# The products x = kv q as six matmuls in natural layout, q split behind one float32 turn through DRAM, h in two banks

## Chip, cores, metric

One core of one Trainium2 chip runs the whole program. The metric is the device time in microseconds (us) of one execution; lower is better. Times below are of the kernel before the change.

## What is computed

The reference is an attention with its softmaxes taken apart, followed by an expert layer (8 batches, 8 heads, 576 positions, 64 columns a head; all float32):

```
q_s = softmax(q, axis=-1);  k_s = softmax(k, axis=2)      # k over the positions
kv  = einsum('bhsd,bhse->bhde', k_s, v)
x   = einsum('bhsd,bhde->bhse', q_s, kv)                  # -> 4608 tokens x 512
h   = x @ w_in                                            # 512 x 2048
g   = s * relu(h)**2 + b
out = g @ w_out                                           # 2048 x 512
```

## The kernel before

**Precision.** A float32 product is made of three products of rounded halves: a value is split into high (rounded to the matmul's type fp32r) and low (the rest), and high·high + high·low + low·high are added in a bank of PSUM.

**Tokens in blocks.** Each batch has 512 main tokens and 64 left ones; the left ones of the eight batches make a ninth block. Batch b's x is block b. The layer runs in steps t = 16·block + f: step t makes h (12 matmuls of 512 columns), TensorE's next 12 matmuls add the step before to the output ("o", written `acc`). Between h and o of a step stand, in this order, ACT's relu into `r`, DVE's square, ACT's `gh` and DVE's `gl`. `r` has one buffer and h one bank. Blocks 0 to 4 run so, in steps 0 to 79. Blocks 5 to 8 run as two pairs, with seven products of half size instead of eight (`bankU`, `bankV`); their x is staged first and cast into the weights' old places (`w<-stage`, b_cast).

**Attention under the layer.** Batches 0 and 1 are done at the start in another way. For batches 2 to 7 (units u = 8 to 31, two heads each; pr = u // 2) every unit's x is made between the layer's steps: `k_late`, `q_late`, `kv_late`, `x_late`. A unit's q passes through ACT's exp (tile `qe`, two buffers), DVE, GpSimd and a 32x32 transpose, then is split in two halves, both are written to DRAM (`turned`) and read back in another order into `spare` (`part()`, one buffer for all units), which TensorE reads. The two halves stand there side by side on 64 + 64 partitions, and one matmul over 128 partitions with 128 weight columns makes two partial sums of a head on the two halves of the output partitions; `evict` copies one half on ACT and adds the other on DVE. A unit takes four such matmuls (2 heads x 2 ranges of 320 and 256 columns).

**Where x goes.** For batches under AHEAD = 3, x is split straight into the layer's tile (`x_tile`). That of later ones goes to DRAM (`xs`); for batches 3 and 4, `x_back` reads it back in two pieces of 512 KB each, and ACT and DVE split it. The layer's tiles have two buffers, so block b's tile is free after h of step 16·(b-1) - 1.

**Order.** All engines execute in a fixed order, written by a planner (`Order`): each work item is an Op with an engine, a planned cost, a due time in steps, names it needs and gives, and buffers it takes and frees; `late=` adds an allowance in us to what it needs. An engine that reaches an instruction whose inputs aren't there waits, and so does all that stands behind it. `a_sums` (GpSimd sums of weights for the pairs) are due from DUE_S on, PACE_S steps apart.

Of the kernel before, what the change touches and what calls it, by code (L numbers as in the profile page):

```python
# [25 lines left out]
def attention_moe(ctx: ExitStack, tc: tile.TileContext, q, k, v, w_in, w_out, s, b, out):  # L26
    nc = tc.nc
# [16 lines left out]
    AHEAD = min(3, FIRST)  # L44
# [546 lines left out]
    def q_late(u):  # L591
# [64 lines left out]
    def kv_late(pr):  # L656
        us = (2 * pr, 2 * pr + 1)
        due = begin(pr)
        tag = "big" if paired(pr // 2) else "sm"
        yield Op("PE", 1.52, due - 200, needs=[f"k{u}" for u in us] + [f"v{pr} there"], take=[tag], gives=[f"kv{pr}"], late=WAIT)  # L660

        kt, _, vt = tiles[pr]
        kv = ps.tile([P, 2, 512], F32, name=f"kv_{pr}", tag="big")[:, 0] if tag == "big" else ps.tile([P, 512], F32, name=f"kv_{pr}", tag="sm", bufs=1)
        kv = kv[:, 0:2 * (D + 1)].rearrange("p (u e) -> p u e", u=2)
        heads(kv, by_head(kt).rearrange("p (u h) n d -> p u h n d", u=2), v_at(vt))
        yield Op("DVE", 0.5, due)
        z = small.tile([P, 2], F32, name=f"z_{pr}", tag="z")
        nc.vector.tensor_scalar(z, kv[:, :, D], 1e-9, None, op0=ALU.add)
        nc.vector.reciprocal(z, z)

        kvf = kvfs[pr % 2]
        for h in range(2):
            yield Op("DVE", 0.5, due, needs=[f"x{u - 4}" for u in us] if pr < NP + 2 else [f"kvhl{pr - 2}"], free=[tag] if h else ())
            for g in range(2):
                nc.vector.tensor_tensor(
                    out=kvf[half[g], :, h], in0=kv[half[h], :, 0:D], in1=z[half[h]].unsqueeze(2).to_broadcast([D, 2, D]),
                    op=ALU.mult
                )
        yield Op("ACT", 0.4, due, needs=["mid"] if pr == NP else [f"xp{2 * pr - 1}"])

        t = kv_part().rearrange("p u (a d) -> p u a d", d=D)
        nc.scalar.copy(t[:, :, 0:4:3], kvf)
        yield Op("POOL", 0.76, due, gives=[f"kvhl{pr}"])
        nc.gpsimd.tensor_tensor(out=t[:, :, 1:3], in0=kvf, in1=t[:, :, 0:4:3].bitcast(F32), op=ALU.subtract)

    def x_late(u):

        pr, i = divmod(u, 2)
        bb, hp = divmod(u, NP)
        due = begin(pr)  # L690
        narrow = paired(bb)
        L, M = NT * D, NQ * D
        width = (NT, NQ)
        qs = lambda: part().rearrange("p h (s a n c) -> p h s n a c", s=2, a=2, c=SQ)
        kvhl = lambda: kv_part()[:, i].rearrange("p (h e) -> p h e", h=2)

        def products(a, outs):
            for h in range(2):
                nc.tensor.matmul(outs[h], kvhl()[:, h], qs()[:, h, a, 0:width[a]], start=True, stop=True)

        def wide_bank(a):
            t = ps.tile([P, 2, 512], F32, name=f"xp_{u}_{a}", tag="big")
            return [t[:, h, 0:L] for h in range(2)] if a == 0 else [t[:, 0, h * M:(h + 1) * M] for h in range(2)]

        needs = [f"q{u}", f"kvhl{pr}"] + [f"y{u - 1}"] * i + ([f"h{NFC * (bb - 1) - 1}"] if bb < AHEAD else [])
        y = None

        def y_at(h, a):
            return y.rearrange("p (n s c) -> p s n c", s=2, c=D)[half[h], a, 0:width[a]]

        def spread_out(outs, h, a):
            return outs[h].rearrange("p (n c) -> p n c", c=D)

        def evict(a, outs, free):
            nonlocal y
            yield Op("ACT", (0.84, 0.74)[a], due, take=() if a else ["tmp", "soft"])
            y = y if y is not None else work.tile([P, 2 * L], F32, name=f"y_{u}", tag="tmp", bufs=NTMP)
            for h in range(2):
                nc.scalar.copy(y_at(h, a), spread_out(outs, h, a)[half[1 - h]])
            if not narrow and a == 0:  # L720
                return
            for a_ in ((0, 1) if not narrow else (a,)):
                yield Op("DVE", (0.98, 0.84)[a_], due, free=free if a_ == a else (), gives=[f"y{u}"] if a_ else ())
                for h in range(2):
                    nc.vector.tensor_tensor(
                        out=y_at(h, a_), in0=spread_out(parts[a_], h, a_)[half[h]], in1=y_at(h, a_), op=ALU.add
                    )

        parts = [None, None]
        if narrow:  # L730
            for a in range(2):
                yield Op("PE", 0.3, due - 200, needs=needs if a == 0 else (), take=["big"], gives=[f"xp{u}"] if a else (), late=WAIT if a == 0 else 0.0)
                parts[a] = wide_bank(a)
                products(a, parts[a])
                yield from evict(a, parts[a], ["big"])
        else:
            yield Op("PE", 0.57, due - 200, needs=needs, take=["big", "sm"], gives=[f"xp{u}"], late=WAIT)
            xq = ps.tile([P, 512], F32, name=f"xq_{u}", tag="sm", bufs=1)
            parts = [wide_bank(0), [xq[:, h * M:(h + 1) * M] for h in range(2)]]
            for h in range(2):  # L740
                for a in range(2):
                    nc.tensor.matmul(parts[a][h], kvhl()[:, h], qs()[:, h, a, 0:width[a]], start=True, stop=True)
            for a in range(2):
                yield from evict(a, parts[a], ["big", "sm"])
        if bb < AHEAD:
            xh, xl = [t[:, hp] for t in x_tile(bb)]
            yield Op("ACT", 0.58, due)
            nc.scalar.copy(xh, y[:, 0:TB])
            yield Op("DVE", 0.69, due, gives=[f"x{u}"])
            nc.vector.tensor_tensor(out=xl, in0=y[:, 0:TB], in1=xh.bitcast(F32), op=ALU.subtract)  # L750
            yield Op("SP", 0.4, due, kb=32, free=["tmp", "soft"], gives=[f"left{u}"])
            nc.sync.dma_start(xleft[:, hp, bb * LEFT:(bb + 1) * LEFT], y[:, TB:S])
        else:
            yield Op("SP", 0.4, due, kb=288, free=["tmp", "soft"], gives=[f"xs{u}", f"left{u}"] + [f"x{u}"] * (bb >= FIRST))
            nc.sync.dma_start(xs[bb][:, hp], y[:, 0:S])

    def x_back(bb, k):
# [7 lines left out]
        yield Op("ACT", 1.04, due, late=SLACK)  # L765
# [68 lines left out]
    def ring_loads():  # L834

        for i in range(len(PAIRS)):
            for p in range(HP):
                for m, k in enumerate(TURN):
# [3 lines left out]
                    needs += [f"kv{2 * FIRST + 1}" if ahead else f"h{FIRST * NFC - 1}"] * (i == 0)  # L842
# [568 lines left out]
```

## Time and profile before

| | us |
|---|---|
| three runs: median (lowest to highest) | 871.23 (868.63 to 871.85) |
| the profiled execution's own time | 870.1 |
| its span, first to last instruction | 868.2 |
| TensorE (PE) busy | 842.8 (97%) |
| VectorE (DVE) busy | 593.9 (68%) |
| ScalarE (ACT) busy | 439.7 (51%) |
| GpSimd (POOL) busy | 197.9 (23%) |

The span is 1.9 us shorter than the execution's own time; sums below are made on the span. TensorE works through a fixed list nearly without a break, so the time is its list's length plus its waits: a change shows where it lengthens the list and where it takes or adds a wait.

### The profile page before, as it was taken

The page shows a single profiled execution, that of the slowest core. Times are in us where ns is not written, and L with a number is a line of the kernel's source. Part 1 is how long each engine was busy: PE and PEld are TensorE (multiplying, and loading weights), DVE is VectorE, ACT ScalarE, POOL GpSimd, SP SyncE. Part 2 cuts the span into 40 slices and gives each one's busy share as a digit, 9 for nine tenths or more (in the row PEclk, how much of TensorE's full clock was granted, in tenths as well). Part 3 has the DMA queues.
Part 4 walks back from the last instruction along what each step waited for, and adds up shares of the span by engine and source line. Part 5 has one row for each costly group of instructions (what it writes and reads, how often), then busy time and mean ns, then how long its engine had stood idle before and what let it go on. Part 6 is the DMA issues. An engine that isn't in the chain of part 4 may idle for free.

```text
span 868.2 us, 12561 instructions
## 1 busy us (share of the span) xinstructions
PE 842.8 (97%) x4358; PEld 691.7 (80%) x4358; DVE 593.9 (68%) x940; ACT 439.7 (51%) x720; POOL 197.9 (23%) x233
## 2 busy tenths in 40 slices
PE   7999999999999899999999988999999999999998
PEld 6688888888878687878888776888888888888886
DVE  6999977898978697979764589755457234444430
ACT  5998644544543445455455575544446243333520
POOL 1000012222213351655634478100022000000000
PEclk9999999999999899999999999999999999999999
DMA  9999255676796787686753658996584256555521
GB/s 268 317 383 313 71 157 178 160 183 145 168 218 154 172 225 200 183 239 161 220 162 82 178 138 234 290 291 198 174 242 159 74 164 187 171 152 156 166 72 49
DMA packets 175828, 161.82 MB, mean 186 GB/s; under 512 B 56468, under 2 KB 143508, under 8 KB 175764
## 3 DMA queue, kind: packets, MB, share of 16 engines
q1 hardware_dynamic: 174612, 159.89, 65.2%
q10 hardware_dynamic: 1152, 1.11, 0.4%
q8 instruction: 35, 0.57, 0.3%
q14 instruction: 29, 0.24, 0.1%
HBM read 106.43 MB, written 54.54 MB: 185 GB/s over the span
## 4 chain that ended last, share of the span: by engine, by line
PE 75%; DMA 8%; DVE 6%; issue 4%; POOL 3%; SPq 3%; ACT 1%; ACTq 0%; POOLq 0%; DVEq 0%
PE acc L1199 31%; PE h L1136 17%; PE bankU L938 9%; PE bankV L938 7%; PE last L1115 5%; PE kv L317 2%; DMA back<-xs 2%; DMA aset<-S 1%; DMA area<-in_v_dram 1%; POOL S L811 1%; DMA xs<-y 1%; POOL S L815 1%; DMA spare<-turned 1%; DMA turned<-area 1%; DMA area<-in_q_dram 1%
## 5 line engine op out<-in xcount | busy, mean ns | idle before, releaser
L1199 PE MATMUL acc<-w,gh 128*128 128x512 f32 x1024 | 317.8, 391 | 0.6 <-ACT gh L1169 0.6
L1136 PE MATMUL h<-x,w 128*128 128x512 f32 x960 | 240.7, 396 | 5.6 <-ACT r L1161 4.9
L1199 PEld LDWEIGHTS acc<-w,gh 128*128 128x128 f32 x1024 | 190.3, 188 | 39.9 <-ACT gh L1169 1.0
L1136 PEld LDWEIGHTS h<-x,w 128*128 128x128 f32 x960 | 180.4, 190 | 45.1 <-ACT r L1161 6.4
L1199 PE MATMUL acc<-w,gl 128*128 128x512 f32 x512 | 200.4, 391 | 6.8 <-DVE gl L1171 5.2
L1199 PEld LDWEIGHTS acc<-w,gl 128*128 128x128 f32 x512 | 96.1, 188 | 29.8 <-DVE gl L1171 6.7
L1161 ACT ACTIVATE r<-h 128x512 f32<-128x512 f32 x80 | 47.7, 596 | 100.9 <-PE h L1136 90.7
L938 PE MATMUL bankU<-w,ring 128*128 128x512 f32 x378 | 96.1, 389 | 0.0
L938 PEld LDWEIGHTS bankU<-w,ring 128*128 128x128 f32 x378 | 70.7, 188 | 14.6 <-ACT stage L1020 0.2
L1174 DVE SCALAR_TENSOR_TENSOR r<-r,sb 128x512 f32<-128x512 f32 x69 | 60.1, 871 | 29.8 <-ACT r L1161 29.4
L938 PE MATMUL bankV<-w,ring 128*128 128x512 f32 x282 | 71.7, 390 | 0.2 <-DVE stage L1022 0.2
L1176 ACT ACTIVATE gh<-r,sb 128x512 fp32r<-128x512 f32 x69 | 50.0, 724 | 31.0 <-DVE r L1174 30.7
L938 PEld LDWEIGHTS bankV<-w,ring 128*128 128x128 f32 x282 | 52.9, 188 | 11.6 <-DVE stage L1022 0.6
L1178 DVE SCALAR_TENSOR_TENSOR gl<-r,sb,gh 128x512 fp32r<-128x512 f32 x69 | 55.6, 805 | 6.4 <-ACT gh L1176 5.6
L600 POOL TENSOR_TENSOR area<-area,qm 128x640 f32<-128x640 f32 x24 | 33.9, 1413 | 82.8 <-DVE qm L598 82.4
L1022 DVE TENSOR_TENSOR rows<-bankV,rows 128x512 f32<-128x512 f32 x30 | 20.7, 691 | 39.4 <-ACT rows L1020 19.4
L1030 DVE SCALAR_TENSOR_TENSOR rows<-rows,sb 128x512 f32<-128x512 f32 x40 | 31.3, 785 | 20.7 <-ACT rows L1024 14.9
L617 POOL TENSOR_TENSOR qe<-qe,qr 128x640 f32<-128x640 f32 x24 | 33.0, 1377 | 54.0 <-issue 23.4
L811 POOL TENSOR_TENSOR S<-S 128x128 f32<-128x128 f32 x64 | 39.1, 612 | 4.5
L910 POOL TENSOR_TENSOR stage<-stage 128x1024 f32<-128x1024 f32 x8 | 21.6, 2695 | 73.6 <-DMA spilt<-rows 62.6
L1115 PE MATMUL last<-w,w 128*128 128x512 f32 x168 | 38.2, 389 | 0.0
L1115 PEld LDWEIGHTS last<-w,w 128*128 128x128 f32 x168 | 31.5, 188 | 6.5
(166 smaller groups left out, 1066.2 us busy)
## 6 DMA issues: line engine op xcount, KB each, us to landing
ring<-aset SPq DMA_DIRECT2D x110, 256.0 KB, 3.0
spare<-turned SPq DMA_DIRECT2D x48, 320.0 KB, 6.3
st<-in_moe_w_in_dram SPq DMA_DIRECT2D x16, 512.0 KB, 7.7
st<-in_moe_w_out_dram SPq DMA_DIRECT2D x16, 512.0 KB, 8.5
out_dram<-o SPq DMA_DIRECT2D x16, 512.0 KB, 3.6
aset<-S SPq DMA_DIRECT2D x32, 256.0 KB, 5.1
turned<-qe SPq DMA_DIRECT2D x24, 320.0 KB, 3.8
turned<-area SPq DMA_DIRECT2D x24, 320.0 KB, 4.3
```

What stands on the lines that cost most here:

```text
L600: nc.gpsimd.tensor_tensor(out=qt, in0=qt, in1=bc(qm, [P, 2, NT, D]), op=ALU.subtract)
L617: nc.gpsimd.tensor_tensor(out=qe_, in0=qe_, in1=qr, op=ALU.mult)
L811: nc.gpsimd.tensor_tensor(out=o, in0=x, in1=y, op=op)
L938: nc.tensor.matmul(out_, w[:, a, c * P:(c + 1) * P], slot(k, c)[:, b_], start=k in (0, 1, 3) and n == 0, stop=n == 5, skip_group_check=True)
L1030: nc.vector.scalar_tensor_tensor(out=r, in0=r, scalar=s_col, in1=r, op0=ALU.mult, op1=ALU.mult)
L1115: nc.tensor.matmul(banks[j], g[:, js], w_, start=(f == 0 and n == 0), stop=(f == NFC - 1 and n == 2))
L1136: nc.tensor.matmul(hp_, w[:, j, c, :], x[:, c, :], start=(c == 0 and i == 0), stop=(c == NP - 1 and i == 2))
L1161: nc.scalar.activation(r, hp_, AF.Relu)
L1174: nc.vector.scalar_tensor_tensor(out=r, in0=r, scalar=s_col, in1=r, op0=ALU.mult, op1=ALU.mult)
L1176: nc.scalar.activation(gh, r, AF.Identity, bias=b_col)
L1178: nc.vector.scalar_tensor_tensor(out=gl, in0=r, scalar=b_col, in1=gh.bitcast(F32), op0=ALU.add, op1=ALU.subtract)
L1199: nc.tensor.matmul(acc[blk, j // 2][:, j % 2], g[:, js], w_, start=(f == 0 and i == 0), stop=(f == NFC - 1 and i == 2))
```

## The change

- **q**: the transposed q goes to DRAM whole, as one float32 tensor (320 KB a unit, in one DMA, not twice 320 KB in two) and comes back in two DMAs of 160 KB into its old tile `qe`, not into `spare`. Only then ACT makes the high half and DVE the low one, both into `spare`. `qe` is held until then.
- **x**: `kv` is a block-diagonal 128x128 matrix for both heads, in a high and a low copy; a unit is six matmuls (three products for 320 columns, three for 256) that end as finished sums in one pair of banks (`big`). No halves are added; ACT copies the sums, and for direct batches DVE subtracts from them. The products and `kv` no longer use the bank `sm`.
- **h**: odd steps from 17 on put h into `sm`, even ones into `h`.
- **AHEAD** is 4: batch 3's x is split straight into its tile, and has no `x_back`; its products must wait for h of step 31.
- **Order**: ACT's copy of `x_back` has an allowance of 10 us (before SLACK, 3); `a_sums` are due from step 34, 1.9 apart (before 38, 2.4); units of batch 7 start after the pairs' first product (before step 72); a block is staged in two DMAs; odd pr of batch 7 has a k tile of its own.

```diff
-    AHEAD = min(3, FIRST)
+    AHEAD = min(4, FIRST)
...
         nc.vector.transpose(out=tb, in_=qe.rearrange("p h t n r -> p (h t n r)"))
-        high = qe.rearrange("p h t n r -> p (h t n r)")
-        yield Op("ACT", 0.72, due)
-        nc.scalar.copy(high.bitcast(F32R), tb)
-        yield Op("DVEp", 0.82, due)
-        nc.vector.tensor_tensor(out=tb, in0=tb, in1=high, op=ALU.subtract)
-        yield Op("SP", 0.8, due, kb=640, take=["turned"], free=["qe"], gives=[f"q{u} turned"])
...
-        for l, t in enumerate((high, tb)):
-            nc.sync.dma_start(turned[u][l].rearrange("h p e -> p h e"), t.rearrange("p (h e) -> p h e", h=2))
...
+        yield Op("SP", 0.4, due, kb=320, take=["turned"], gives=[f"q{u} turned"])
+        turned[u] = dram.tile([2, P, 2 * NT * SQ], F32, name=f"turned_{u}", tag="turned", bufs=2)
+        nc.sync.dma_start(turned[u].rearrange("h p e -> p h e"), tb.rearrange("p (h e) -> p h e", h=2))
+        yield Op("SP", 1.3, due, needs=[f"q{u} turned"], free=["turned"], late=SLACK, kb=320, gives=[f"q{u} back"])
...
+        for h in range(2):
+            nc.sync.dma_start(t[half[h]].rearrange("p (a e) -> p a e", a=4), src[h])
+        yield Op("ACT", 0.72, due, needs=[f"q{u} back", f"xp{u - 1}" if u > 2 * NP else "mid"], late=SLACK)
+        high, low = [part()[:, l] for l in range(2)]
+        nc.scalar.copy(high, t)
+        yield Op("DVEp", 0.82, due, free=["qe"], gives=[f"q{u}"])
+        nc.vector.tensor_tensor(out=low, in0=t, in1=high.bitcast(F32), op=ALU.subtract)
...
+        xp = ps.tile([P, 2, 512], F32, name=f"xp_{u}", tag="big")
+        qs = part().rearrange("p l (s a n c) -> p l s n a c", s=2, a=2, c=SQ)
+        for s_, n in enumerate((NT, NQ)):
+            for k, (l, m) in enumerate(((0, 0), (1, 0), (0, 1))):
+                nc.tensor.matmul(xp[:, s_, 0:n * D], kv_part()[:, l, i], qs[:, m, s_, 0:n], start=k == 0, stop=k == 2)
...
+            yield Op("ACT", 0.84, due, take=["tmp", "soft"], free=["big"])
+            y = work.tile([P, S], F32, name=f"y_{u}", tag="tmp", bufs=NTMP)
+            nc.scalar.copy(order(y[:, 0:TB]), x)
+            nc.scalar.copy(y[:, TB:S], left)
...
-        yield Op("ACT", 1.04, due, late=SLACK)
+        yield Op("ACT", 1.04, due, late=10.0)
...
+    def h_bank(t):
+        return "sm" if t > NFC and t % 2 else "h"
...
-    DUE_S, PACE_S = 38, 2.4
+    DUE_S, PACE_S = 34, 1.9
...
-        there = [f"w{NFC - 1} 1 there"] if pr == NP else [f"h{FIRST * NFC - 8}"] if paired(pr // 2) else []
+        there = [f"w{NFC - 1} 1 there"] if pr == NP else ["P1 0 0"] if paired(pr // 2) else []
```

The order at three places. First ACT's around the relu of step 36 (`r_36`): before, the split of the first piece of batch 3 read back from DRAM (`back_3_0`) stands ahead of it.

```order
L1161 ACTIVATE r_35_2563<-h_35_2539 128x512
L719 COPY y_14_2579<-xp_14_0_2569 64x5x64 x2
L1176 ACTIVATE gh_35_2564<-r_35_2563,sb_85 128x512
L767 CAST x_3_2595<-back_3_0_2588 128x1024
L719 COPY y_14_2579<-xq_14_2568 64x4x64 x2
L587 ACTIVATE area_87<-area_87 128x640
L604 ACTIVATE qe_17_2617<-area_87 128x640
L1161 ACTIVATE r_36_2627<-h_36_2597 128x512
```

Now ACT has there, of q, the copy that waits for unit 15's q to come back (`spare<-qe_15`), behind `r_36`.

```order
L1128 ACTIVATE r_35_2564<-h_35_2515 128x512
L587 ACTIVATE kalt0_1383<-kalt0_1383 128x640
L1143 ACTIVATE gh_35_2565<-r_35_2564,sb_85 128x512
L587 ACTIVATE kalt0_1383<-kalt0_1383 128x640
L1128 ACTIVATE r_36_2625<-h_36_2595 128x512
L1143 ACTIVATE gh_36_2626<-r_36_2625,sb_85 128x512
L632 CAST spare_1380<-qe_15_2396 128x640
L604 ACTIVATE qe_17_2664<-area_87 128x640
L1128 ACTIVATE r_37_2669<-h_37_2644 128x512
```

What moved: `back_3_0` and the halves' copies are gone; the wait for DRAM on ACT is now that of `qe_15`. In the same way each of the 24 units has one `spare<-qe` copy. Second, TensorE's order at unit 14's x, before:

```order
L1199 MATMUL acc_2_0_2465<-w_2_505,gl_34_2523 128x512
L742 MATMUL xp_14_0_2569<-spare_1381 128x320
L742 MATMUL xq_14_2568<-spare_1381 128x256
L742 MATMUL xp_14_0_2569<-spare_1381 128x320
L742 MATMUL xq_14_2568<-spare_1381 128x256
L1199 MATMUL acc_2_0_2465<-w_2_505,gh_34_2522 128x512 x2
```

And now:

```order
L1166 MATMUL acc_2_2_2437<-w_1_485,gl_33_2422 128x512
L691 MATMUL xp_14_2506<-spare_1380 128x320 x3
L691 MATMUL xp_14_2506<-spare_1380 128x256 x3
L1103 MATMUL h_35_2515<-x_2_1697,w_3_573 128x512 x12
```

Four matmuls have become six of the same two widths, half a step earlier. Unit 12 stands after h of step 31 (before in step 29's o), unit 27 after h of step 63 (before after o of step 69). Third, DVE's order shortly ahead of the pairs, from `gl` of step 75 to that of step 78, before: casts for the pairs (`w<-stage`) among batch 7's q (`area`, `qe_28`, `qe_29`) and k.

```order
L1171 TENSOR_TENSOR gl_75_4849<-r_75_4847,gh_75_4848 128x512
L626 TENSOR_TENSOR area_87<-area_87,qe_28_4811 128x640
L895 TENSOR_TENSOR w_8_814<-stage_0_4281,w_8_814 128x512
L621 STREAM_TRANSPOSE area_87<-qe_29_4830 128x640
L895 TENSOR_TENSOR w_9_798<-stage_0_4281,w_9_798 128x512
L895 TENSOR_TENSOR w_12_1008<-stage_0_4281,w_12_1008 128x512
L1171 TENSOR_TENSOR gl_76_4899<-r_76_4897,gh_76_4898 128x512
L626 TENSOR_TENSOR area_87<-area_87,qe_29_4830 128x640
L544 TENSOR_TENSOR area_87<-area_87,misc_90 128x640 x2
L895 TENSOR_TENSOR w_13_1173<-stage_0_4281,w_13_1173 128x512
L1171 TENSOR_TENSOR gl_77_4947<-r_77_4945,gh_77_4946 128x512
```

And now, to `gl` of step 78:

```order
L1138 TENSOR_TENSOR gl_75_4704<-r_75_4702,gh_75_4703 128x512
L1138 TENSOR_TENSOR gl_76_4737<-r_76_4735,gh_76_4736 128x512
L859 TENSOR_TENSOR w_12_1007<-stage_0_4251,w_12_1007 128x512
L1138 TENSOR_TENSOR gl_77_4772<-r_77_4770,gh_77_4771 128x512
L859 TENSOR_TENSOR w_13_1172<-stage_0_4251,w_13_1172 128x512
L859 TENSOR_TENSOR w_4_653<-stage_0_4251,w_4_653 128x512
L1138 TENSOR_TENSOR gl_78_4808<-r_78_4806,gh_78_4807 128x512
```

Batch 7's q and k have left this place for the time after the pairs' start; the first of the fourteen casts stands behind `gl` of step 65.

## Rows read from the trace of the kernel before

**Rows 1.** The page's head and busy times, share of the span, instructions.

```profile
span 868.2 us, 12561 instructions
PE 842.8 (97%) x4358; PEld 691.7 (80%) x4358; DVE 593.9 (68%) x940; ACT 439.7 (51%) x720; POOL 197.9 (23%) x233
```

**Rows 2.** Waits of PE: us in total, times, longest us.

```profile
PE acc L1199 <- DVE gl L1171: 5.2, 3, 2.6
PE h L1136 <- ACT r L1161: 4.9, 3, 2.8
...
PE acc L1199 <- DVE gl L1178: 1.5, 1, 1.5
PE kv L317 <- issue: 1.1, 2, 0.7
PE xq L742 <- DVE kvf L675: 0.8, 1, 0.8
...
PE acc L1199 <- ACT gh L1169: 0.6, 1, 0.6
```

**Rows 3.** Timeline of PE: start, us, work [idle before it <-releaser].

```profile
259.06 4.61 PE L1136 MATMUL h<-x,w 128*128 128x512 f32 x12 [1.88 <-ACT r L1161]
...
293.75 1.65 PE L1136 MATMUL h<-x,w 128*128 128x512 f32 x3 [2.79 <-ACT r L1161]
296.11 2.44 PE L317 MATMUL kv<-area,kalt 128*64 128x65 f32 x40 [0.71 <-issue]
```

**Rows 4.** Windows: us, PE, PEld, DVE, ACT, POOL busy (instructions), PEclk, DMA share, GB/s.

```profile
259.50:262.90 3.40, 3.40 (x10) 2.66 (x9) 3.27 (x7) 1.35 (x2) 0.20 (x1) 0.50 0.22 87
293.60:300.40 6.80, 5.94 (x48) 4.66 (x49) 6.06 (x13) 1.95 (x4) 2.06 (x2) 0.50 0.57 171
262.00:480.00 218.00, 211.92 (x1135) 173.82 (x1134) 165.75 (x280) 106.26 (x184) 103.68 (x124) 0.98 0.68 181
```

**Rows 5.** Timeline of ACT, the two pieces of batch 3 read back.

```profile
255.28 1.05 ACT L767 CAST x<-back 128x1024 fp32r<-128x1024 f32 x1 [4.08 <-DMA back<-xs]
...
292.16 1.04 ACT L767 CAST x<-back 128x1024 fp32r<-128x1024 f32 x1 [6.05 <-DMA back<-xs]
```

**Rows 6.** Waits of ACT, the row of all four pieces.

```profile
ACT x L767 <- DMA back<-xs: 16.0, 4, 6.0
```

**Rows 7.** Timeline of DVE ahead of the pairs.

```profile
496.13 2.30 DVE L532 TENSOR_TENSOR sb<-sb 64x8 f32<-64x8 f32 x1
...
503.87 2.13 DVE L895 TENSOR_TENSOR w<-stage,w 128x512 fp32r<-128x512 f32 x1
```

**Rows 8.** Timeline of PE, unit 8's four matmuls and what follows.

```profile
161.92 0.31 PE L742 MATMUL xp<-spare 128*128 128x320 f32 x1
162.07 0.28 PE L742 MATMUL xq<-spare 128*128 128x256 f32 x1
...
162.46 0.86 PE L1136 MATMUL h<-x,w 128*128 128x512 f32 x3
```

**Rows 9.** Groups by form of PE: count | busy us, mean ns | idle before.

```profile
L742 PE MATMUL xp<-spare 128*128 128x320 f32 x40 | 11.7, 313 | 0.1
```

**Rows 10.** Groups of DVE from 230 to 430 us: the adding of halves.

```profile
L725 DVE TENSOR_TENSOR y<-xp,y 64x320 f32<-64x320 f32 x24 | 11.7, 488 | 0.5
...
L725 DVE TENSOR_TENSOR y<-xq,y 64x256 f32<-64x256 f32 x24 | 10.1, 422 | 0.5
```

**Rows 11.** Instructions of L1174, DVE's square: least/median/largest ns.

```profile
L1174 DVE SCALAR_TENSOR_TENSOR r<-r,sb x69: 653/750/1693, 39.4 to 464.7; 128x512 f32<-128x512 f32 x69
```

**Rows 12.** Window of L1174 alone: us, DVE busy (instructions), PEclk, DMA share, GB/s.

```profile
262.00:480.00 218.00, 30.79 (x33) 0.98 0.68 181
```

**Rows 13.** DMA issues: count, KB each, median us to landing.

```profile
spare<-turned SPq DMA_DIRECT2D x48, 320.0 KB, 6.3
...
back<-xs SPq DMA_DIRECT2D x4, 512.0 KB, 5.4
```

**Rows 14.** DMAs of the tile `turned`, both ways.

```profile
DMA to landing us min/median/max: 2.3/5.2/9.1
```

More of the change, by code (lines that the diff above doesn't have):

```diff
@@ L671, in kv_late @@
         kvf = kvfs[pr % 2]
+        yield Op("DVE", 0.6, due, needs=[f"x{u - 4}" for u in us] if pr < NP + 2 else [f"kvhl{pr - 2}"], free=["big"])
         for h in range(2):
[L673 to L678, printed above, removed]
@@ L679, in kv_late @@
-        yield Op("ACT", 0.4, due, needs=["mid"] if pr == NP else [f"xp{2 * pr - 1}"])
-        t = kv_part().rearrange("p u (a d) -> p u a d", d=D)
-        nc.scalar.copy(t[:, :, 0:4:3], kvf)
+            nc.vector.tensor_tensor(
+                out=kvf[half[h], :, h], in0=kv[half[h], :, 0:D], in1=z[half[h]].unsqueeze(2).to_broadcast([D, 2, D]), op=ALU.mult
+            )
+        yield Op("ACT", 0.42, due, needs=["mid"] if pr == NP else [f"xp{2 * pr - 1}"])
+        high, low = [kv_part()[:, l] for l in range(2)]
@@ L683, in kv_late @@
+        kvf = kvf.rearrange("p u h d -> p u (h d)")
+        nc.scalar.copy(high, kvf)
         yield Op("POOL", 0.76, due, gives=[f"kvhl{pr}"])
-        nc.gpsimd.tensor_tensor(out=t[:, :, 1:3], in0=kvf, in1=t[:, :, 0:4:3].bitcast(F32), op=ALU.subtract)
+        nc.gpsimd.tensor_tensor(out=low, in0=kvf, in1=high.bitcast(F32), op=ALU.subtract)
     def x_late(u):
@@ L690, in x_late @@
         due = begin(pr)
[L691 to L744, printed above, removed]
+        yield Op(
+            "PE", 0.83, due - 200, needs=[f"q{u}", f"kvhl{pr}"] + ([f"h{NFC * (bb - 1) - 1}"] if bb < AHEAD else []), take=["big"], gives=[f"xp{u}"], late=WAIT
+        )
@@ L745, in x_late @@
         if bb < AHEAD:
             xh, xl = [t[:, hp] for t in x_tile(bb)]
[L747 to L750, printed above, removed]
+            yield Op("ACT", 0.62, due)
+            nc.scalar.copy(order(xh), x)
+            yield Op("DVE", 0.7, due, gives=[f"x{u}"])
+            nc.vector.tensor_tensor(out=order(xl), in0=x, in1=order(xh.bitcast(F32)), op=ALU.subtract)
@@ L751, in x_late @@
+            yield Op("ACT", 0.22, due, take=["tmp", "soft"], free=["big"])
+            y = work.tile([P, LEFT], F32, name=f"y_{u}", tag="tmp", bufs=NTMP)
+            nc.scalar.copy(y, left)
             yield Op("SP", 0.4, due, kb=32, free=["tmp", "soft"], gives=[f"left{u}"])
-            nc.sync.dma_start(xleft[:, hp, bb * LEFT:(bb + 1) * LEFT], y[:, TB:S])
+            nc.sync.dma_start(xleft[:, hp, bb * LEFT:(bb + 1) * LEFT], y)
         else:
+            yield Op("ACT", 0.84, due, take=["tmp", "soft"], free=["big"])
@@ L1158, in step @@
             hp_ = next(parts)
-        yield Op("ACT", 0.54, t - 2, needs=["sb there"] * (t == 0), take=["r", "g"], free=["h"])
+        yield Op("ACT", 0.54, t - 2, needs=["sb there"] * (t == 0), take=["r", "g"], free=[h_bank(t)])
         r, gh, gl = g_tiles(t)
@@ L1316, in reload_late @@
         else:
[L1317 removed]
+            gone = [f"kv{pr - 1 if pr == NP else pr - 2}"]
         def k_():
```

75 lines of the change are left out of this document (37 added, 38 removed).

## The prediction

> **What bounds the kernel.** I read the page's busy times first, since they say which engine's list the time is. TensorE is busy 842.8 of 868.2 us, VectorE 68% [rows 1]: the time is TensorE's list plus its waits. So the next view is the list of TensorE's waits. Past the start, which the change leaves alone, it has few, and they add to 14.1 us: 5.2, 4.9, 1.5, 1.1, 0.8, 0.6 [rows 2], and of the 1.1 about 0.4 belongs to another k. Then I asked the timeline where the long ones stand: h waits for ACT's relu 1.88 us at 259 and 2.79 us at 293.75, and 0.71 us more pass ahead of a kv at 296 [rows 3]. After both the granted clock stands at 0.50, that is 1.2 of 2.4 GHz, for 3.4 and 6.8 us [rows 4]. ACT's timeline says why its relu was late: it stood behind the split of batch 3's x, which had waited 4.08 and 6.05 us for `back<-xs` [rows 5]. All four such splits waited, 16.0 us together [rows 6]. The waits for `gl` of L1171 are those of steps 70 to 79; there DVE works on batch 7's k and q and on casts at once, with single instructions of 2.30 and 2.13 us [rows 7]. The reader is to see that TensorE's losses have two roots: an engine in order that waits for DRAM, and a crowd ahead of the pairs.
>
> **What the change costs on TensorE.** Four matmuls start at 161.92 and the next one after them at 162.46: 0.54 us a unit. The first, 320 columns, takes 0.15 until the next starts [rows 8], so one of 256 takes 0.12 (half of 0.54 less 0.15). Six cost 3 x 0.15 + 3 x 0.12 = 0.81, so 0.27 more. There are 24 units: 20 have the 40 of 320 columns at L742, two each [rows 9]; batch 7's four have the same widths. 24 x 0.27 = **+6.5 us**, all on the path, since TensorE has no free time to hide it. Three products into one bank follow each other as h's do, so I see no reason for another rate; the lower bound is that of the columns alone (576 more a unit), the same within 0.3 us in all.
>
> **What it removes.**
> - Batch 3's read-back is gone with both its splits on ACT. Idle 1.88 + 2.79 + 0.71 = 5.38 [rows 3]. At half clock TensorE worked 3.40 + 5.94 us [rows 4], of which half is lost: 4.67. Together **-10.0 us**.
> - Batch 4's read-back stays, but ACT's split stands 7 us later in the order (allowance 10 instead of 3). It landed in 5.4 us at the median [rows 13] and kept ACT idle for 4 us on average [rows 6], so 7 us cover it. It stood ahead of the waits of 1.5 and 0.8 us and of 4.9 - 1.88 - 2.79 = 0.2 [rows 2]: **-2.5 us**. If the cover fails they stay.
> - The crowd: batch 7's k and q leave DVE, ACT and GpSimd around steps 75 to 79 (the third place of the order) and follow the pairs' start; the casts begin at step 65. Waits of 5.2 and 0.6 us [rows 2]: **-5.8 us**. What hides batch 7 afterwards is the pairs' first half, and none of these waits is at bankU or bankV; its last unit stands at the o of step 89, before at that of 87, with the second pair's first product after that of 109.
>
> That is -18.3. Also DVE loses the adding of halves, 2 x 0.488 + 2 x 0.422 = 1.82 us a unit [rows 10], and ACT half of its copies. These lie beside TensorE and count for nothing by themselves; they give slack to the next term. So does the second bank for h: it lets TensorE run one h ahead of a late relu, but `r` has still one buffer and `gl` must still come in time, so I give it no sum of its own.
>
> **What it adds.** Each unit now has a place on ACT where q's return is waited for (`spare<-qe`), and behind it stand relu and `gh` of the next steps, for which TensorE waits. Before, the same return was waited for by TensorE, with allowances of 3 us (SP) and 2.5 (TensorE), and none of its waits is for `spare` [rows 2]. Now there are 3 at SP and 3 at ACT, and half the bytes (before twice 320 KB, 6.3 us to landing at the median [rows 13]; out and back ranged from 2.3 to 9.1 [rows 14]). So I expect few waits, and small ones. But units also stand closer: u12 to u27 lie within steps 31 to 63, before within 29 to 69. From below the cost is 0; from above it is many such waits (first rival). I take one event like that at 259: 1.88 idle and 3.40 / 2 of clock, **+3.6 us**, because outside the two roots the list leaves only 0.4 us of waits past the start [rows 2] at today's spacing. Batch 3's units must wait for h of step 31; they need to be done by step 48, and u15 stands at the o of step 36, so 11 steps are left, and I cost this at nothing; if that cover is gone, u12's wait is one more event.
>
> **Sum.** 868.2 - 18.3 + 6.5 + 3.6 = 860.0 us of span; with the 1.9 us between span and time, 861.9. The profiled execution took 870.1, the median of the runs is 871.2, with 3.2 us between lowest and highest; I forecast **862 us** for the median and don't add the difference, which is within that scatter.
>
> **Rivals.**
> *The wait moves to ACT (slower).* Place: the 24 copies `spare<-qe`. For it: all four copies that waited on ACT for a DRAM trip with the same two allowances of 3 us did wait, 4 us on average [rows 6], and two of them cost TensorE 1.88 + 1.70 = 3.6 and 2.79 + 0.71 + 2.97 = 6.5 us [rows 3, 4], 5.0 on average. Against it: those were 512 KB pieces, and the q trip, with more bytes than now, has cost TensorE nothing. It decides from three such events on beyond my one: 862 + 3 x 5.0 = 877 us. With two it is 872, no change.
>
> *GpSimd and DVE get in each other's way (no change).* The weight sums are due over 15 x 1.9 = 28.5 steps, before 36. GpSimd was busy 103.68 of 218 us there, 48% [rows 4]; packed so, 61%. DVE's square takes 0.653 us at least [rows 11] and 30.79 / 33 = 0.933 in that stretch [rows 12]: 0.28 lost at 48%, so 0.36 at 61%, 0.08 more. With two such instructions in each of 30 steps and some three in each of 16 units, 108 x 0.08 = 9 us more on DVE, against 16 x 1.82 = 29 us less: this would cost nothing. From above, the largest square lost 1.693 - 0.653 = 1.04; at 61% that is 0.63, 0.35 more than now, 38 us, so DVE would gain nothing and its busy share, 165.75 / 218 = 76% now, would pass 80%. `gl` would then come late at some steps; two more events of 3.6 to 5.0 us give 869 to 872. I hold the lower price for the nearer one, as it is a mean of 33.
> The Trainium skill, SBUF — State Buffer, section "Who interferes with whom", says that a VectorE instruction with two SBUF inputs is held by a GpSimd instruction that reads SBUF, for all of that instruction, rather than both being slowed. The trace agrees in kind: a subtract-like one on 64x8 elements took 2.30 us [rows 7]. By this rule the new `low = q - high` and the squares lose whole GpSimd instructions, and the time is this rival's.
>
> *The change does less than it says (no change).* The waits at 259 and 293 would come back at `acc`, because what was late is `gl` as much as the relu, held up by k and q of later units. For it: the read-back is the last of several things in ACT's queue. Against it: ACT was idle in front of it. Half of the 18.3 would stay: 871.
>
> **How the numbers follow.** A measurement here tells about 0.5% (4.4 us) from no change; below 866.9 counts as faster, above 875.6 as slower. The forecast, with 0 to 2 events of new waiting, spans 857 to 867: 0.70. GpSimd and DVE: 0.10. Less than it says: 0.11. Waits on ACT: 0.09. So faster 0.71 (a small part of the rivals falls under 866.9), same 0.20, slower 0.09. The range goes from 856 (no new wait and a little more) to 872, which takes in the two middle rivals and leaves out the slow one and the tail below. The likeliest case by itself has 857 to 867.
>
> **What would show each step.** Six matmuls a unit, starts 0.15 and 0.12 apart, 0.81 in all. In TensorE's waits: none for ACT's relu over 1 us, no stretch at clock 0.50 between 250 and 310 us, and under 2 us for `gl` ahead of the pairs. `x<-back` twice, not four times, with little idle time ahead. ACT's waits show `spare<-qe` behind the DMA: a total under 10 us says the slower rival is wrong, some 30 with relu waits on TensorE says it is right. DVE busy about 594 - 24 x 1.82 = 550 us; GpSimd's sums done well before step 79. The prediction is wrong if the six matmuls take more than 0.9 us a unit, or if TensorE waits for `spare`, `acc` or h more than 8 us past the start.

## The result, and the profile after

| | before | after |
|---|---|---|
| median of the runs, us | 871.54 (4 runs, 868.63 to 871.95) | 857.62 (4 runs, 857.39 to 858.25) |
| profiled execution, us (span) | 870.1 (868.2) | 858.25 (856.5) |
| TensorE / VectorE busy, us | 842.8 / 593.9 | 842.6 / 536.6 |

The ratio is 0.9844, with an interval of 0.9821 to 0.9867: faster by 1.6%, 13.9 us by the medians and 11.8 by the two profiled executions, whose rows are compared below. The forecast was 862, with 856 to 872 as its range.

I read the views in the order of before. First the head of the page and its busy times, against [rows 1].

```profile
span 856.5 us, 12467 instructions
...
PE 842.6 (98%) x4406; PEld 696.7 (81%) x4406; DVE 536.6 (63%) x822; ACT 413.4 (48%) x666; POOL 199.4 (23%) x234
```

TensorE has 48 matmuls more and the same busy time; 11.7 us of span are gone. So what fell is its idle time, 868.2 - 842.8 = 25.4 before and 13.9 now; in its busy time the longer products and the end of half clock, both priced further down, cancel out. Next its list of waits. Three of its rows are of the layer and of the late units, against [rows 2].

```profile
PE xp L691 <- DVE kvf L668: 1.7, 2, 0.9
...
PE acc L1166 <- DVE gl L1145: 0.7, 1, 0.7
PE h L1103 <- DVE x L469: 0.7, 1, 0.7
```

The last belongs to 38 us, the layer's start; so past the start 1.7 + 0.7 = 2.4 us stand against the 14.1 of before. Neither a wait for relu nor one ahead of the pairs is there. The windows, against [rows 4], with the place of batch 3's old read-backs first and that of the crowd last:

```profile
250.00:310.00 60.00, 58.27 (x365) 47.69 (x365) 49.80 (x81) 27.03 (x47) 37.88 (x42) 1.00 0.65 165
262.00:480.00 218.00, 215.55 (x1145) 178.43 (x1144) 144.99 (x212) 97.78 (x166) 121.57 (x136) 1.00 0.51 147
480.00:545.00 65.00, 65.00 (x288) 53.81 (x288) 30.00 (x49) 36.70 (x58) 11.55 (x8) 1.00 0.49 146
```

The granted clock is 1.00 where it had been 0.50 twice, and from 480 to 545 TensorE is busy without a gap. GpSimd's share from 262 to 480 rose to 121.57 / 218 = 56%. DVE's square alone in that window, against [rows 12], and the six matmuls of two units with what follows, in the timeline of PE:

```profile
262.00:480.00 218.00, 29.20 (x33) 1.00 0.51 147
```

```profile
162.70 0.96 PE L691 MATMUL xp<-spare 128*128 128x320 f32 x6
163.50 2.21 PE L1103 MATMUL h<-x,w 128*128 128x512 f32 x9
...
172.53 0.96 PE L691 MATMUL xp<-spare 128*128 128x320 f32 x6
173.33 0.62 PE L1166 MATMUL acc<-w,gh 128*128 128x512 f32 x2
173.79 0.39 PE L1166 MATMUL acc<-w,gl 128*128 128x512 f32 x1
```

From the first of the six to what follows 0.80 us pass both times; 0.81 had been worked out. The square's mean is 29.20 / 33 = 0.885 us, before 0.933.

Last, ACT: its waits and timeline, where batch 4 is read back, against [rows 5, 6].

```profile
ACT x L727 <- DMA back<-xs: 6.5, 2, 4.3
```

```profile
370.87 1.05 ACT L727 CAST x<-back 128x1024 fp32r<-128x1024 f32 x1 [4.29 <-DMA back<-xs]
371.83 0.72 ACT L1143 ACTIVATE gh<-r,sb 128x512 fp32r<-128x512 f32 x1
374.80 1.05 ACT L727 CAST x<-back 128x1024 fp32r<-128x1024 f32 x1 [2.26 <-DMA back<-xs]
```

Batch 4's two pieces still keep ACT waiting, 6.5 us (before 3.76 and 2.08, 5.8). Behind them TensorE's timeline had two waits before, and has one now:

```profile
340.55 3.02 PE L1136 MATMUL h<-x,w 128*128 128x512 f32 x12 [0.22 <-ACT r L1161]
...
345.55 0.50 PE L1199 MATMUL acc<-w,gl 128*128 128x512 f32 x1 [1.52 <-DVE gl L1178]
```

```profile
372.77 0.61 PE L1166 MATMUL acc<-w,gh 128*128 128x512 f32 x2
374.10 0.50 PE L1166 MATMUL acc<-w,gl 128*128 128x512 f32 x1 [0.71 <-DVE gl L1145]
374.44 0.62 PE L1166 MATMUL acc<-w,gh 128*128 128x512 f32 x2
```

The reader is to see an ACT that waits as long as before and a TensorE that hardly notices: only the 0.71 us for `gl` at 374 is behind it. For q's return (`qe<-turned`) ACT has no row among its waits.

### The profile page after: what moved, and what is told of

The parts are those of the page before. It is cut to its first block, busy times and chain, and to the rows that moved or that the text cites. A ratio compares the mean times of both kernels' runs of the same rounds, so it can differ in the third digit from the quotient of the medians.

```text
span 856.5 us, 12467 instructions
## 1 busy us (share of the span) xinstructions
PE 842.6 (98%) x4406; PEld 696.7 (81%) x4406; DVE 536.6 (63%) x822; ACT 413.4 (48%) x666; POOL 199.4 (23%) x234
## 3 DMA queue, kind: packets, MB, share of 16 engines
q10 hardware_dynamic: 1152, 1.11, 0.4%
## 4 chain that ended last, share of the span: by engine, by line
PE 90%; DMA 5%; DVE 3%; issue 1%; ACT 0%; SPq 0%; ACTq 0%; DVEq 0%
PE acc L1166 39%; PE h L1103 23%; PE bankU L902 10%; PE bankV L902 8%; PE last L1079 5%; PE xp L691 2%; PE kv L317 2%; DMA area<-in_q_dram 2%; DMA st<-in_moe_w_out_dram 1%; DMA raw<-in_q_dram 1%; DMA maxima<-sb 1%; DMA back<-xs 1%; DVE r L1141 0%; PE xp L460 0%; DMA misc<-maxima 0%
## 5 line engine op out<-in xcount | busy, mean ns | idle before, releaser
L1103 PE MATMUL h<-x,w 128*128 128x512 f32 x960 | 235.8, 392 | 0.8 <-DVE x L469 0.7
L1103 PEld LDWEIGHTS h<-x,w 128*128 128x128 f32 x960 | 178.6, 188 | 38.4 <-DVE x L469 1.4
L1128 ACT ACTIVATE r<-h 128x512 f32<-128x512 f32 x80 | 47.8, 597 | 132.7 <-PE h L1103 128.9
L1141 DVE SCALAR_TENSOR_TENSOR r<-r,sb 128x512 f32<-128x512 f32 x69 | 57.9, 838 | 54.0 <-ACT r L1128 53.8
L1145 DVE SCALAR_TENSOR_TENSOR gl<-r,sb,gh 128x512 fp32r<-128x512 f32 x69 | 58.9, 854 | 11.9 <-ACT gh L1143 11.1
L600 POOL TENSOR_TENSOR area<-area,qm 128x640 f32<-128x640 f32 x24 | 35.9, 1498 | 75.6 <-DVE qm L598 52.9
```

The source lines that it names most:

```text
L600: nc.gpsimd.tensor_tensor(out=qt, in0=qt, in1=bc(qm, [P, 2, NT, D]), op=ALU.subtract)
L1103: nc.tensor.matmul(hp_, w[:, j, c, :], x[:, c, :], start=(c == 0 and i == 0), stop=(c == NP - 1 and i == 2))
L1128: nc.scalar.activation(r, hp_, AF.Relu)
L1141: nc.vector.scalar_tensor_tensor(out=r, in0=r, scalar=s_col, in1=r, op0=ALU.mult, op1=ALU.mult)
L1145: nc.vector.scalar_tensor_tensor(out=gl, in0=r, scalar=b_col, in1=gh.bitcast(F32), op0=ALU.add, op1=ALU.subtract)
```

## The experiments

**The theory** after the result: the gain is batch 3's read-back, taken off ACT's queue; the six products cost what their columns cost; the waits of the crowd (DVE's work ahead of the pairs) went with batch 7's move. **Rivals:** the gain is the new shape of x and q (lighter DVE and ACT, half the bytes), or batch 7's place, or the second bank. Each run was timed beside the kernel before on its own chip (medians 869.8, 869.7 and 871.0 on three chips); ratios are against that. The kernel after was timed on a chip where the kernel before takes 871.5, so a difference from "after" of 1 to 2 us is not told apart from that between chips.

### The read-back alone, and put back

`e1_before_ahead4`, the old kernel with two numbers of the change:

```diff
-    AHEAD = min(3, FIRST)
+    AHEAD = min(4, FIRST)
...
-        yield Op("ACT", 1.04, due, late=SLACK)
+        yield Op("ACT", 1.04, due, late=10.0)
```

> The kernel before with two edits alone: AHEAD is 4 (batch 3's x goes straight to its tile, no read-back) and ACT's split of batch 4's read-back has an allowance of 10 us. If the two read-backs caused the waits of TensorE (my theory), the time falls by 10.0 + 2.5 us, from 871.5 to about 859, with no stretch at clock 0.50 between 250 and 310 us. If the gain of the whole change lies in the new shape of the products (no adding of halves, less on VectorE), it falls by no more than 3 us, to 868 or above.

Measured: 857.39 (856.62 to 857.8), ratio 0.9861 (0.9836 to 0.9886), as good as the whole change. Its waits of PE past the start:

```profile
PE xq L742 <- DVE kvf L675: 1.4, 1, 1.4
PE acc L1199 <- DVE gl L1171: 1.2, 2, 0.6
PE h L1136 <- ACT r L1161: 1.1, 1, 1.1
PE kv L317 <- issue: 1.1, 2, 0.7
...
PE kv L317 <- DVE y L725: 0.7, 2, 0.5
```

No clock of 0.50 is left between 8 and 854 us. That and the missing waits at 259 to 296 are the 10.0 us of the prediction's first term; the other 2.4 of 12.4 are the balance of waits that moved: those ahead of the pairs fell from 5.2 to 1.2 though batch 7 kept its place, while the 1.4 for `kvf` and others are new or longer.

`e2_after_readback` is the reverse, the new kernel with both numbers as they were (AHEAD 3, SLACK).

> The changed kernel with AHEAD back at 3 and ACT's allowance for a read-back at 3 us: both read-backs are there as before, everything else is new. My theory: the waits at the relu come back, 10.0 + 2.5 us, 857.6 becomes about 870. Rival: the new slack (second bank for h, less work on VectorE) hides them, and the time stays under 861.

Measured: 869.67 (866.84 to 871.38), ratio 0.9997 (0.9977 to 1.0017): the whole gain is lost. First ACT's timeline, then PE's:

```profile
237.60 1.05 ACT L727 CAST x<-back 128x1024 fp32r<-128x1024 f32 x1 [7.68 <-DMA back<-xs]
238.55 0.59 ACT L1128 ACTIVATE r<-h 128x512 f32<-128x512 f32 x1
...
240.61 0.72 ACT L1143 ACTIVATE gh<-r,sb 128x512 fp32r<-128x512 f32 x1 [0.56 <-DVE r L1141]
```

```profile
241.38 1.00 PE L1166 MATMUL acc<-w,gh 128*128 128x512 f32 x2 [1.96 <-ACT gh L1143]
243.62 0.80 PE L1166 MATMUL acc<-w,gl 128*128 128x512 f32 x1 [1.25 <-DVE gl L1145]
```

This is the chain of [rows 3, 5] again: DRAM, ACT's split, relu, then TensorE, and the clock at 0.50 for 6.8 us. But the wait has moved from h to `acc`: with a second bank TensorE makes the next h meanwhile (12 matmuls from 236.54), and then waits for `gh` of the step before. In that point the third rival of the prediction was right.

### Is it the read-back, or ACT's wait for it?

`e5_before_late10` was to tell the place of ACT's wait from the read-back as such: the old kernel with `late=10.0` alone. `e6_after_readback_long` is the new one with AHEAD 3 and the 10 kept.

> The kernel before with one edit alone: ACT's split of a read-back has an allowance of 10 us in the order, not 3; AHEAD stays 3, so both read-backs are there. If the loss comes from where ACT waits and not from the read-back as such, the allowance alone gives nearly all of the gain, 857 to 860. If batch 3's read-back must go for it, only batch 4's part comes, 2.5 us: 867 to 869.

> The changed kernel with AHEAD back at 3 but the allowance of 10 us kept. If the place of ACT's wait is the cause, it stays within 2 us of the change, 857 to 859. If the read-back as such costs (its copies, its DMA traffic, the tile's lateness), it is 861 or more.

Measured: 870.49, ratio 1.0002 (0.9985 to 1.0018), and 869.24, ratio 0.9992 (0.9979 to 1.0005). The allowance does nothing in either: `late` is added to what an Op *needs*, and ACT's Op in `x_back` names nothing that it needs, so not one instruction moves and the split is planned right behind the issue of its load. What these two runs give is how well a null edit repeats: `e6_after_readback_long` is `e2_after_readback` again, 869.24 against 869.67.

The allowance acts once the split needs what the load gives. `e9_before_real10` is the old kernel, AHEAD still 3, with this; `e11_before_ahead4_real10` adds AHEAD 4, and `e10_after_real10` makes the edit in the new kernel.

```diff
-        yield Op("SP", 0.65, due - 2, needs=[...], take=["tmp", "soft", "slow"], kb=512, late=SLACK)
+        yield Op("SP", 0.65, due - 2, needs=[...], take=["tmp", "soft", "slow"], kb=512, late=SLACK, gives=[f"back {bb} {k}"])
...
-        yield Op("ACT", 1.04, due, late=SLACK)
+        yield Op("ACT", 1.04, due, needs=[f"back {bb} {k}"], late=10.0)
```

> The kernel before, AHEAD 3, with the allowance of 10 us made to act: ACT's split now names the landing that it needs, and stands later in the order (behind the relu of step 37, not 36, for batch 3's first piece). The edit of the allowance alone, which left the order of all engines as it was, gave nothing. If the cause is where ACT waits for DRAM, most of the 12 us come without any change of AHEAD: 858 to 862. If the read-back as such costs, it stays above 867.

> The kernel before with AHEAD 4 and the allowance made to act for batch 4's read-back. With AHEAD 4 alone TensorE waits 1.1 us for a relu at 375 and 0.4 for gl at 404; the first stands behind a read-back on which ACT waited 5.5 us. If that goes, 856; no gain (857.4) if the wait comes back at another instruction.

> The changed kernel with the allowance for batch 4's read-back made to act in the same way. ACT still waits 6.5 us for it in the changed kernel and TensorE 0.7 us behind that: the most it can bring is 1 us, 857 to 858; above 860 if the later x of block 4 is missed by step 64.

In `e9_before_real10` and `e11_before_ahead4_real10` the edit also moves other work: a split that stands later holds its buffer longer, GpSimd's weight sums, which need one too, come later, and so part of those for blocks 5 to 8 is made from weights that the pairs' casts have already overwritten. In the former one split of x, batch 4's first by the planned order, is made from other data as well. Number and form of the instructions are the same, but these two don't compute the whole result, and a kernel that did could be slower.

`e9_before_real10` came to 863.31 (11 runs, 857.72 to 867.86), ratio 0.9925 (0.9899 to 0.995): some 1 us above the 858 to 862 expected, and below the 867 that would have spoken for the read-back as such. All four pieces are read back through DRAM as before, and ACT's timeline shows their splits with no wait; batch 3's two:

```profile
267.55 1.05 ACT L767 CAST x<-back 128x1024 fp32r<-128x1024 f32 x1
...
300.51 1.04 ACT L767 CAST x<-back 128x1024 fp32r<-128x1024 f32 x1
```

TensorE's waits for relu fell from 4.9 to 0.2 us, and no clock of 0.50 is left between 8 and 515 us. So at the read-back it is ACT's in-order wait that costs TensorE its time, not the trip. Of the 12.4 us of `e1_before_ahead4` 7.7 come back. What is left stands elsewhere, in its waits of PE, and the longer of its two for `stage` has the same form in ACT's timeline, with GpSimd in the place of DRAM:

```profile
PE bankU L938 <- ACT stage L1020: 4.0, 2, 3.0
...
PE acc L1199 <- ACT gh L1169: 2.3, 1, 2.3
```

```profile
560.25 0.62 ACT L813 CAST S<-S 128x512 fp32r<-128x512 f32 x1 [5.61 <-POOL S L811]
560.77 0.58 ACT L1020 COPY stage<-bankU 128x512 f32<-128x512 f32 x1
```

ACT waits 5.61 us for a late weight sum (`S`), and the copy that TensorE needs stands behind it.

`e11_before_ahead4_real10` missed what was expected: 866.46 (862.83 to 869.35), ratio 0.9955 (0.9935 to 0.9975), 9 us slower than `e1_before_ahead4`. ACT has no read-back wait, but TensorE has one of 4.41 us ahead of the pairs and one of 3.93 within them (their first product is at 521 us), each with a stretch of 6.8 us at half clock. PE's timeline, and the windows of those stretches:

```profile
502.53 0.80 PE L1199 MATMUL acc<-w,gl 128*128 128x512 f32 x1 [4.41 <-DVE gl L1171]
...
564.80 0.80 PE L938 MATMUL bankU<-w,ring 128*128 128x512 f32 x1 [3.93 <-ACT stage L1020]
```

```profile
501.60:508.40 6.80, 5.87 (x14) 4.62 (x15) 6.14 (x6) 4.86 (x8) 4.70 (x4) 0.50 0.80 195
563.10:569.90 6.80, 5.10 (x12) 4.05 (x13) 2.93 (x4) 2.96 (x5) 1.92 (x3) 0.50 1.02 269
```

The second is again a copy on ACT behind a cast that waited for a late weight sum, 6.31 us.

`e10_after_real10`: 857.06 (856.35 to 857.71), ratio 0.9845 (0.9818 to 0.9871). ACT's read-back wait is gone there too, and the median is 0.6 us less, within the scatter of the runs. Batch 4's read-back is worth no more in the new kernel.

### The parts of the new shape

`e3_after_one_h`: `h_bank` always gives "h".

> The changed kernel with h in one bank for all steps, the order of TensorE's work unchanged. My theory gives the second bank no sum of its own: within 1 us of 857.6. Rival: the second bank is what hides late relus; then TensorE waits for r again and the time is 862 or more.

858.85 (857.83 to 861.95), ratio 0.9887 (0.9859 to 0.9914). One wait of PE of 0.90 us comes back at 376.75, right behind batch 4's second piece; its row, with a smaller one, is `PE h L1103 <- ACT r L1128: 1.1, 2, 0.9`. By the trace the second bank is worth about 1 us, there; the medians differ by 1.2, within the scatter, and the ratios by 0.0043, some 3.7 us. So its size is open between these, below the 862 of its rival.

`e4_after_four` leaves out the third product, kv high · q low, so that a unit has four matmuls again.

```diff
-            for k, (l, m) in enumerate(((0, 0), (1, 0), (0, 1))):
...
+            for k, (l, m) in enumerate(((0, 0), (1, 0))):
...
```

> The changed kernel without the third product of x (kv high by q low), so four matmuls a unit and not six; the low half of q is made but not used. If the products lie wholly on TensorE's path, 24 x 0.27 us come off: 857.6 becomes about 851. If other engines or waits set the pace there, the time stays at 855 to 858.

852.96 (852.49 to 854.46), ratio 0.9818 (0.9792 to 0.9843), where 851 stood. Span 850.4 and TensorE 836.6 us busy, 6.1 and 6.0 less than after. Two matmuls a unit, 24 times, are 48, and each takes 0.15 or 0.12: 6.5 worked out. TensorE's list is shorter by nearly that. How much of it reaches the time is less sure: the profiled execution is the lowest of this run and was the highest of the kernel after, the medians differ by 4.7 us, and the ratios by 0.0026, some 2.3 us.

`e7_after_batch7_early` puts batch 7 of the new kernel back to where it was:

```diff
...
-        return pr > NP and pr % 2
+        return NP < pr < 2 * FIRST + 2 and pr % 2
...
-        there = [...] if pr == NP else ["P1 0 0"] if paired(pr // 2) else []
+        there = [...] if pr == NP else [f"h{FIRST * NFC - 8}"] if paired(pr // 2) else []
...
```

> The changed kernel with batch 7's loads allowed from step 72 on as before (k tiles and their needs as before with it). My prediction's third term says that the crowd of batch 7's k and q and the casts ahead of the pairs costs 5.8 us: 857.6 becomes 862 to 863. The rival: the lighter x work leaves room for it there and it costs under 1.5 us.

862.47 (860.22 to 863.26), ratio 0.9906 (0.9891 to 0.9922): 4.8 us slower than after by the medians, 3.6 by the profiled executions; near the 5.8 of the prediction's term, and in another place. Between 480 and 545 TensorE is busy 64.95 of 65 us. The loss is at 408, in the timelines of ACT and PE:

```profile
407.12 1.05 ACT L727 CAST x<-back 128x1024 fp32r<-128x1024 f32 x1 [3.77 <-DMA back<-xs]
```

```profile
408.85 0.73 PE L1166 MATMUL acc<-w,gh 128*128 128x512 f32 x2 [1.72 <-ACT gh L1143]
410.26 0.77 PE L1166 MATMUL acc<-w,gl 128*128 128x512 f32 x1 [0.68 <-DVE gl L1145]
```

with 3.4 us at clock 0.50 behind it. With batch 7's earlier start batch 4's read-back moved from 371 and 375 to 402 and 407, and ACT's wait for its second piece reached TensorE once more.

`e8_four_products_best` is `e1_before_ahead4` with batch 7 moved as in the new kernel: four products, no read-back, no crowd.

> The kernel before (four products, q split ahead of DRAM, h in one bank) with AHEAD 4, the allowance of 10 us and batch 7 after the pairs' first product; none of the six products, the float32 turn or the second bank. If those three give nothing by themselves and the products cost 24 x 0.27 us, this beats the changed kernel by about 4 us: 853. If the new shape of x carries part of the gain, it stays at 857 or above.

It missed: 859.72 (857.78 to 860.92), ratio 0.9878 (0.9861 to 0.9895), where 853 stood. The crowd is gone (TensorE busy 65.00 of 65 us from 480 on), but `PE acc L1199 <- DVE gl L1080: 3.4, 2, 2.3` is new, at 655 and 662, where the second pair's casts now meet what moved. The timelines of DVE and GpSimd there:

```profile
651.83 2.84 DVE L1080 SCALAR_TENSOR_TENSOR gl<-w,sb,gh 128x512 fp32r<-128x512 f32 x1
...
658.66 2.87 DVE L1080 SCALAR_TENSOR_TENSOR gl<-w,sb,gh 128x512 fp32r<-128x512 f32 x1
```

```profile
648.58 5.55 POOL L910 TENSOR_TENSOR stage<-stage 128x1024 f32<-128x1024 f32 x2 [52.52 <-DMA out_dram<-o]
655.42 5.56 POOL L910 TENSOR_TENSOR stage<-stage 128x1024 f32<-128x1024 f32 x2 [1.29 <-DVE w L895]
```

`gl` takes 2.8 us in place of 0.74 while GpSimd adds two stages. What batch 7's move gave at the pairs' start was given back later.

`e12_after_no_allowance` takes ACT's allowance of 3 us for q's return away (`late=SLACK` becomes `late=0.0` at the copy into `spare`). It is the test of the slower rival.

> The changed kernel with no allowance on ACT's copy that waits for q's return from DRAM (3 us before). This is the slower rival made on purpose: if such waits cost TensorE 3.6 us and more each, some of the 24 do so and the time rises to 862 or more. If q's return has room anyway, it stays at 857 to 859.

863.34 (861.72 to 864.59), ratio 0.9915 (0.9893 to 0.9937), 5.7 us slower than after. ACT's waits and its two longest:

```profile
ACT spare L632 <- DMA qe<-turned: 8.4, 5, 3.1
...
ACT x L727 <- DMA back<-xs: 5.3, 1, 5.3
```

```profile
374.57 0.73 ACT L632 CAST spare<-qe 128x640 fp32r<-128x640 f32 x1 [3.14 <-DMA qe<-turned]
...
562.59 0.73 ACT L632 CAST spare<-qe 128x640 fp32r<-128x640 f32 x1 [2.96 <-DMA qe<-turned]
```

Behind these two TensorE waits 0.65 us (377.36) and 0.82 us (563.87), where the rival had priced 5 an event. The largest single part of the 5.7 is again batch 4's read-back, whose 5.33 us of ACT at 346 to 352 are followed by TensorE waits of 1.57 and 1.11 us. The rival's mechanism is real and needs no more than an allowance of 3 us to stay away; its price was too high.

## Why the prediction was right, and where it was not

Direction, range and main cause held: faster, inside 856 to 872, and batch 3's read-back as the largest term. The size was off: 8.2 us of span were foreseen and 11.7 measured. Two terms make most of that: the new waits (+3.6, measured +1.7), and what a wait costs beyond its idle time (0.27 us each, last section; 8 waits fewer are about -2.2), which was not counted at all. Batch 4's term came out 0.7 smaller. The crowd's and batch 4's terms together are 8.3 of the 18.3 us removed, and neither came about in the way that was named: that their sums are nearly right is luck.

- **Batch 3's read-back, -10.0.** Right: its waits and its half clock are gone. Alone in the old kernel its end is worth 12.4 (`e1_before_ahead4`), put back in the new one it costs 12.0 (`e2_after_readback`); what is above 10.0 is waits elsewhere that move along. `e9_before_real10` shows that it is ACT's wait and not the trip.
- **Batch 4's read-back, -2.5 by an allowance of 10.** The step was wrong. The allowance moves nothing (`e5_before_late10`), so the split doesn't stand 7 us later and nothing covers the trip: ACT waits 6.5 us against 5.8 before, and yet TensorE's idle time behind it fell from 1.52 + 0.22 to 0.71 (the 0.8 that the term also has, for `kvf` at 389, is gone). The second bank accounts for one of these waits (`e3_after_one_h`); I take the lighter DVE for the rest, which no run tells apart.
- **The second bank, no sum.** About 1 us by the trace, at that one place.
- **The crowd, -5.8 by batch 7's place.** The waits are gone, but batch 7's place is not what took them away. They are also gone with batch 7 early (`e7_after_batch7_early`), and 1.2 of 5.2 are left in the old kernel without batch 3's read-back. What batch 7's place is worth, 4.8 us by the medians, shows at batch 4's read-back. What sets the crowd's waits is open. The last ten of the pairs' fourteen casts start on DVE at 502 before and 496 in `e11_before_ahead4_real10`, at 487 in `e1_before_ahead4`. A rival that no run tests alone is GpSimd's weight sums, which the change made due earlier (DUE_S, PACE_S). Their last instruction starts at 546 before, 531 in `e1_before_ahead4`, 564 in `e11_before_ahead4_real10`, and at 484 after, 486 in `e7_after_batch7_early`, 516 in `e8_four_products_best`; the waits around the pairs' start follow that row as well as the casts, and two of the late ones hang on such a sum by ACT's timeline.
- **Six products, +6.5.** Right in the list: 0.80 a unit, and 6.0 us of TensorE's busy time in `e4_after_four`; of the time, 4.7 by the medians and 2.3 by the ratios.
- **New waits, +3.6.** Too high. In place of an event with half clock there are 0.81 and 0.92 us for `kvf` at 279 and 306, 1.7 together; the clock stayed at 1.00.
- **Rivals.** Waits on ACT for q's return: not in this kernel, but 3 us of allowance away. Its evidence was misread: the four copies of the read-back had an allowance on ACT that moved nothing, where that of `spare<-qe` acts, so they were no model for it; with an acting one (`e9_before_real10`, `e10_after_real10`) ACT doesn't wait for them either. GpSimd and DVE: the share rose to 56% (61% foreseen) and the square became faster, 0.885 us; not in this kernel, but shown in `e8_four_products_best`. Less than it says: the wait at `acc` is real (`e2_after_readback`), but only with the read-back in.
- **DVE busy**, 550 foreseen, is 536.6; where the other 13 us went was not followed up.

By the rows the sum is now: idle past the start -11.7 (14.1 to 2.4), half clock -4.7, products 24 x (0.80 - 0.54) = +6.2, and about -2.2 for 8 waits fewer: -12.4, against -11.7 of span. The 0.7 between them I can't place; the kernel after also has a half-clock stretch of 3.4 us at 12 us, ahead of all that changed, whose price I don't know.

As for the change as a whole: its expensive part, the six products, is paid back by what goes with it, and one number, AHEAD, gives the same time in the old kernel (857.39; the other number of `e1_before_ahead4` moves nothing). No version here is clearly below 857 us with the whole computation; `e10_after_real10` with 857.06 ties.

## What to carry to other kernels

Look first for an in-order engine that waits for a DRAM round trip and has the critical engine's next input queued behind it: its price is the idle time, the clock where it falls after it (here after waits of 1.88 and 2.79 us, not after the 2.56 us ahead of the pairs), and the waits that follow later in the order. Before an allowance or a due time of a planner gets a price, see in the order that it moves an instruction. And price every wait at its place in the *new* order, since here each of three edits that were to take one away or bring one back (`e7_after_batch7_early`, `e8_four_products_best`, `e11_before_ahead4_real10`) had its gain or loss somewhere else.

## What the runs showed of the hardware

**A DVE instruction is held to the end of a GpSimd one.** DVE's and GpSimd's timelines of the kernel after:

```profile
336.38 1.72 DVE L1141 SCALAR_TENSOR_TENSOR r<-r,sb 128x512 f32<-128x512 f32 x1
```

```profile
336.28 1.27 POOL L617 TENSOR_TENSOR qe<-qe,qr 128x640 f32<-128x640 f32 x1 [6.04 <-ACT r L1128]
```

GpSimd ends at 337.55, the square at 338.10, 0.55 later; at its least it takes 0.653 and at the median 0.75 in all. In `e11_before_ahead4_real10` a `gl` of 2.90 us from 508.67 ends 0.55 after GpSimd's 2.62 us from 508.40, and in `e8_four_products_best` the `gl` from 651.83 ends 0.54 after GpSimd's two. In the kernel after, every one of the 12 squares above 0.9 us ends 0.55 us (0.546 to 0.555) after a GpSimd instruction on two tensors. A square that starts first is not held: the one at 278.95, 0.22 ahead of a GpSimd instruction of 1.57 us, takes 0.65. The Trainium skill, SBUF — State Buffer, section "Who interferes with whom", says that a VectorE instruction with two SBUF inputs contends with a GpSimd instruction that reads SBUF, that the shared pair of ports is an exclusive lock, and that the order of issue decides who blocks; these rows agree. So a late `gl` costs up to the length of one GpSimd instruction, and that is what to keep short ahead of a critical one, more than GpSimd's share.

**A wait costs more than its idle time.** A matmul of 512 columns is counted 0.39 us busy, and the next starts 0.23 after it ([rows 8] show the same overlap). The last one before a wait counts its full 0.39, of which 0.16 overlap with nothing; and the first one behind a wait is followed after 0.34, not 0.23. In TensorE's rows of 372.77 to 374.44 above, three matmuls at 0.23 each would put the fourth at 373.46; it starts at 374.44. So a wait of 0.71 us delays TensorE by 0.98, 0.27 more than its idle time.

**The same ACT wait has many prices.** 7.68 us cost TensorE 1.96 + 1.25 us and 6.8 us at half clock; 3.77 us cost 1.72 + 0.68 and 3.4 at half clock; 4.29 us cost 0.71; 5.52 us in `e1_before_ahead4` 1.14. In these runs it depends on what stands behind the waiting instruction more than on its length.
